# Asking earlier for the tables, spectra and filter of a convolution that runs beside an FFN, with tables and planes in common buffers

## The chip, the cores and the metric

The kernel runs on one core of a Trainium2 chip. The metric is the device time of one execution in microseconds (us); lower is better. A core has five engines that run at the same time and wait for each other through semaphores: TensorE (PE, matrix products), VectorE (DVE), ScalarE (ACT), GpSimd (POOL) and SyncE (SP), which here only issues DMAs. POOL also issues DMAs. PE's weight loads have a row of their own in the profile (PEld).

## The reference

Two blocks follow each other. The first is a long convolution by FFT with an implicit filter (batch 4, sequence 12544, 128 channels); the second is a maxout FFN over all 50176 tokens:

```python
h_filt = (np.maximum(pos_emb @ w1, 0) @ w2) * np.exp(-0.01 * pos)[:, None]
u = x * v
Uf = np.fft.rfft(u, n=2 * S, axis=1)
Hf = np.fft.rfft(h_filt, n=2 * S, axis=0)
y = np.fft.irfft(Uf * Hf[None], n=2 * S, axis=1)[:, :S]
z = (x * y).reshape(B * S, D)                       # D = 128
h = np.maximum(np.maximum(z @ m1, z @ m2), z @ m3)  # d_ff = 768
out = h @ m_out
```

## The kernel before

**Stages.** The transform is split by hand into a short one over 90 frequencies and a long one over 128 points, written as fp32 matrix products. Until about 290 us the kernel computes the filter's spectrum (kept in HBM as `hd`) and convolves batch 0. Then comes a loop over the FFN tiles of batches 0, 1 and 2: 32 tiles a batch, each of 6 slots, so 192 slots a batch. In a slot PE computes one sixth of a tile's FFN (`up`, tile `hps`, then `down`, tile `ops`), and beside it runs a piece of the convolution of the *next* batch. The last batch's FFN, from about 1,770 us on, has nothing beside it.

**What runs beside the FFN.** `conv_steps` makes a plan by hand: a list of steps for each slot. First, in the slots up to about 53, come 32 *units* of the next batch: load (`u_load`, SP), multiply and cut into 16-bit planes (`u_mul`, `u_planes`, POOL), transpose by DMA (`u_dma`, SP), join, first transform (`u_two`, `u_fours`). They fill the tile `spec`. From slot `s0` (58 in batch 2's plan) on come the *pairs*: 45 frequency steps g, two to a start slot, a new pair each 5.1 slots or so. With s for the start slot of a pair:

- `w_load` (L506, DMA at L508 on POOL) brings the tables `wt` of one step, 256 KB; one table serves the forward step g and the inverse step g - 3.
- `q_load` (L512, L520 on SP) brings the spectra `sq` of the two steps of a pair, eight DMAs of 64 KB out of `spec`, two buffers.
- `h_load` (L526, L531 on SP) brings the filter `ht` of the two steps, four DMAs of 256 KB out of `hd`, two buffers.
- `g_quarter` (L537) in slot s: PE multiplies `sq` by `wt` (L547) and, for the inverse of g - 3, `xs` by `wt` (L557).
- `g_fold`, `q_swap`, `q_re`, `q_im`, `q_unfold` in the next slots: ACT, DVE and POOL make `cb` and `xs` of it; `q_re` and `q_im` (DVE, L596) multiply by `ht`, and POOL adds at L599. `q_im` of a pair's second step has, in most pairs, the slot s + 5.
- `g_store` (L580, POOL) writes the inverse step's result to HBM (`zd`).

**Order of the queues.** Each engine executes its instructions in the order in which the program emits them, slot by slot. SP's list holds, besides the above, `t_load` (L776): at each tile's first slot it asks for the tile after the next of `zt` out of `zd` (L782 for batch 0, L789 after it; two buffers), and its first DMA waits until that buffer is read out. On each of the two DMA queues a DMA also waits for the landing of the one eight places before it, whose semaphore it takes over. POOL's list holds the tables' DMAs, the stores of `zd` and of the FFN's output (`ot`), the loads of `xT` and the sums at L599.

The asking steps stand in the plan at these slots: tables and spectra at s - 4, the filter at s - 1. The first pairs have entries of their own (`h_load` of the first two pairs, `w_load` of the first three tables).

Of the kernel before, what the change touches and what calls it, by code (L numbers as in the profile page):

```python
# [10 lines left out]
FP32 = mybir.dt.float32  # L11
I32 = mybir.dt.int32
U16 = mybir.dt.uint16
# [3 lines left out]
P = 128  # L17
# [78 lines left out]
def kernel(  # L96
# [21 lines left out]
    NK = N1 // 2  # L118
# [287 lines left out]

    def u_planes(u):
        a, _ = us.pop(u)
        pl_ = cvp.tile([P, 2, 4, P], U16, tag="pl", name="planes", bufs=3)
        w = pl_[:].rearrange("p h s (e m) -> p h s e m", e=2)  # L410
        nc.gpsimd.memset(pl_[:].rearrange("p h s (e m) -> p (h s e) m", e=2)[:, :, HB:], 0)
        for h in range(2):
            nc.gpsimd.tensor_copy(  # L413
                w[:, h, :, :, 0:HB],
                a[:].bitcast(U16).rearrange("p s (m e h) -> p h s e m", e=2, h=2)[:, h])
        us[u] = pl_
# [87 lines left out]
            fn()  # L504

    def w_load(x):  # L506
        w = wp.tile([P, 2, 2, 2, 64], FP32, tag="w", name="wt")
        nc.gpsimd.dma_start(w[:].rearrange("p a k r m -> p (a k r m)"),  # L508
                            wq_d[x].rearrange("p a f -> p (a f)"))
        ws[x, 0], ws[x - LATE, 1] = w[:, 0], w[:, 1]  # L510
# [153 lines left out]
    def conv_steps(b, done):  # L664


        out = []

        def at(slot, late, fn, *args):
            out.append((slot, late, len(out), fn, args))  # L670

        for u in range(5, done):
            at(2 * (u - 4), 1, u_first, u)
        lead, low, UNIT = (-14, -NT * NF, 0.8) if b > 1 else (6, 0, 0.7)
        share = UNIT * (NU - done - 1)
        per_pair = (END - lead - 11) / (share + (NK + LATE) // 2 * 2 - 2)
        units = []
        for u in range(done, NU):  # L680
            s = (u - done) * UNIT * per_pair + lead
            load_ = max(low, int(s) - 9)
            at(load_, 0, u_load, b, u)
            mul = max(load_ + 2, int(s) - 6)
            at(mul, 0, u_mul, u, nc.gpsimd)
            at(max(mul, int(s) - 5), 0, u_planes, u)
            at(max(mul + 1, int(s) - 4), 0, u_dma, u)
            at(int(s), 0, u_join, u)
            if u % 2:
                on = int(s + 2)  # L690
                at(on, 1, u_two, u - 1)
                at(on + 1, 1, u_fours, u - 1)
                at(on + 2, 1, u_fours, u)
                units.append(on)
        s0 = on + 7

        def start(x):
            return s0 + int(x // 2 * 2 * per_pair)

        load = [0.6] * (NT * NF)  # L700
        for x in range(NK + LATE):
            s = start(x)
            load[s] -= 1.2
            load[s + 1 + x % 2] += 1.4

        def emptiest(among, cost):
            s = min(among, key=lambda i: load[i])
            load[s] += cost
            return s

        plan = []
        busy = {start(x): 2 for x in range(NK + LATE)}
        for x in range(NK + LATE):
            busy.setdefault(start(x) + 1, 1)
        for s in units:
            for k, n in enumerate((1, 3, 9, 2)):
                busy[s - 1 + k] = max(n, busy.get(s - 1 + k, 0))
        for i in range(NT - 1):
            s = i * NF
            last = min((3, 4, 2), key=lambda k: busy.get(s + k, 0))  # L720
            load[s + last] += 0.6
            if s <= s0:
                plan.append((0, 0, last))
                continue
            a = emptiest(range(s, s + 2), 0.7) - s
            plan.append((a, emptiest(range(s + a, s + max(a + 1, last - 1)), 0.7) - s, last))
        plan.append((3, 3, 4))

        for at_, fn, *args in ((11, h_load, 0, 2), (10, h_load, 2, 2),
                               (9, w_load, 0), (9, w_load, 1), (8, w_load, 2)):  # L730
            at(s0 - at_, 0, fn, *args)
        for x in range(NK + LATE):
            s, odd = start(x), x % 2
            g, z = x if x < NK else None, x - LATE if x >= LATE else None
            at(s, 1, g_quarter, g, z)
            at(s + 1 + odd, 0, g_fold, g, z)
            if x > 2:
                at(s - 4, 0, w_load, x)
            if z is not None:
                at(s + 3 + odd, 0, g_store, b, z)  # L740
            if g is None:
                continue
            if g % 2 == 0:
                at(s - 4, 0, q_load, g, min(2, NK - g))
                if g > 2:
                    at(s - 1, 0, h_load, g, min(2, NK - g))
            first = s + 2 + 2 * odd
            at(first, 0, q_swap, g, 0)
            at(first + 1, 0, q_swap, g, 64)
            last = start(x + LATE) - 1  # L750
            a = emptiest(range(first + 1, min(first + 3, last - 1) + 1), 0.7)
            at(a, 0, q_re, g)
            a = emptiest(range(a, min(first + 4, last - 1) + 1), 0.7)
            at(a, 0, q_im, g)
            two = sorted(emptiest(range(a + 1, last + 1), 0.55) for _ in range(2))
            for q in range(2):
                at(two[q], 0, q_unfold, g, q)
        slots = {}
        for s, _, _, fn, args in sorted(out, key=lambda r: r[:3]):
            slots.setdefault(s, []).append((fn, args))  # L760
        return slots, plan, s0
# [288 lines left out]
    for u in range(4, NU, 2):  # L1050
        t = uts.pop(u)
        for v in range(2):
            if u + 4 < NU:
                u_mul(u + 4 + v)
            at = 4 * (u + v)
# [23 lines left out]
    cvp = pro.enter_context(tc.tile_pool(name="cvp0", bufs=3))  # L1079
# [94 lines left out]
    for s in range(NK + 3):  # L1174
# [34 lines left out]
        if s == NK:  # L1209
            unit(0)  # L1210
            pl = sps.tile([P, 512], FP32, tag="pl", name="pl")
# [23 lines left out]
    wp = conv.enter_context(tc.tile_pool(name="wp", bufs=3))  # L1235
    hh = conv.enter_context(tc.tile_pool(name="hh", bufs=2))
    cvp = conv.enter_context(tc.tile_pool(name="cvp", bufs=3))
# [12 lines left out]
    for b in range(1, B):  # L1250
        slots, *rest = conv_steps(b, EARLY if b == 1 else 0)
        plans.append(rest)
        for s, steps in slots.items():
            besides.setdefault((b - 1) * NT * NF + s, []).extend(steps)
# [145 lines left out]
```

## Time and profile before

| | |
|---|---|
| time, median of 3 runs | 2230.89 us (2227.69, 2230.89, 2235.35) |
| profiled execution | 2221.21 us, its span 2219.4 us |
| PE busy | 2194.1 us, 99% of the span |
| DVE, ACT, POOL busy | 1534.6, 1210.9, 1179.0 us |
| loop over the FFN tiles of batches 0 to 2 | about 290 to 1,770 us of the span |
| pairs run in | 447 to 768, 952 to 1,263 and 1,457 to 1,768 us |

All times within the execution count from the start of the span. The profiled execution is one execution with the hardware's profiler on; it took 9.7 us less than the median of the runs without it. A row of a view of waits reads: engine, tile and line that waited, then who ended the wait, the total in us, how many times, and the longest.

### The profile page before, as it was taken

To read this page: it belongs to the slowest core of one execution; us is meant where nothing else is said; L and a number is where in the kernel's file an instruction comes from. 1 tells how busy PE (TensorE), PEld (TensorE's weight loads), DVE (VectorE), ACT (ScalarE), POOL (GpSimd) and SP (SyncE) were. 2 spreads that over 40 slices of the span, in tenths; PEclk is the share of its full clock that TensorE was granted. 3 is DMA by queue.
4 is the path that set the end of the run, shared out by engine and by line. 5 is a ranking of instruction groups with operands and counts; after the bars stand their busy time and mean duration, and the time that the engine had idled before them with its cause. 6 is when DMAs were issued, how large, how long until landed. Compare 5 with 4: busy or idle time off the path is not lost.

```text
span 2219.4 us, 77166 instructions
## 1 busy us (share of the span) xinstructions
PE 2194.1 (99%) x31655; PEld 1297.3 (58%) x31655; DVE 1534.6 (69%) x3293; ACT 1210.9 (55%) x2223; POOL 1179.0 (53%) x1577
## 2 busy tenths in 40 slices
PE   9999999999999999999999999999999999999999
PEld 7988755555555455555555555555555545667776
DVE  5688857677877766667888766677878744554443
ACT  3699845466666555456666555556666622222222
POOL 1166567534455566544444566634454426666665
PEclk9999999999999999999999999999999999999999
DMA  8789999879999898879999999969999722222221
GB/s 196 186 264 311 291 181 196 171 191 233 247 246 241 218 188 175 168 175 245 230 256 231 229 195 178 173 158 252 236 240 238 200 79 58 59 71 69 63 58 24
DMA packets 491332, 411.62 MB, mean 185 GB/s; under 512 B 289406, under 2 KB 407920, under 8 KB 490979
## 3 DMA queue, kind: packets, MB, share of 16 engines
q1 hardware_dynamic: 443689, 274.50, 56.6%
q0 software_dynamic: 45808, 130.25, 21.5%
q8 instruction: 249, 4.08, 0.8%
q10 hardware_dynamic: 1482, 1.93, 0.4%
q14 instruction: 104, 0.85, 0.1%
HBM read 262.85 MB, written 84.67 MB: 157 GB/s over the span
## 4 chain that ended last, share of the span: by engine, by line
PE 84%; DMA 6%; DVE 3%; POOL 3%; issue 2%; SPq 1%; ACT 1%; POOLq 0%; DVEq 0%; ACTq 0%
PE hps L167 42%; PE ops L167 17%; PE ops L903 6%; PE cps L167 3%; PE cps L449 3%; PE ps L176 3%; PE cps L547 3%; PE cps L557 2%; DMA sq<-spec 2%; DMA ht<-hd 2%; DMA zt<-zd 1%; PE ps L167 1%; DMA wt<-wq_const 1%; POOL xt L638 1%; PE last L167 1%
## 5 line engine op out<-in xcount | busy, mean ns | idle before, releaser
L167 PE MATMUL hps<-gt,w_sb 128*64 128x392 f32 (+1 forms) x7672 | 1157.4, 495 | 0.8 <-DVE gt L829 0.7
L839 ACT ACTIVATE hid<-hps 128x392 f32<-128x392 f32 x768 | 382.5, 498 | 762.7 <-PE hps L167 744.9
L167 PEld LDWEIGHTS hps<-gt,w_sb 128*64 128x64 f32 (+1 forms) x7672 | 430.6, 126 | 439.1 <-issue 407.9
L842 DVE TENSOR_TENSOR hid<-hid,hps 128x392 f32<-128x392 f32 x768 | 427.8, 557 | 351.5 <-PE hps L167 335.8
L167 PE MATMUL ops<-hid,wo_sb 128*64 128x392 f32 x2304 | 476.9, 492 | 0.0
L599 POOL TENSOR_TENSOR cb<-cb,xs 128x512 f32<-128x512 f32 x135 | 177.4, 1314 | 404.9 <-DVE xs L596 389.5
L167 PEld LDWEIGHTS ops<-hid,wo_sb 128*64 128x64 f32 x2304 | 165.7, 137 | 213.5 <-issue 213.5
L572 DVE TENSOR_TENSOR cb<-cps,eo 128x512 f32<-128x512 f32 (+1 forms) x288 | 175.1, 649 | 72.8 <-ACT eo L569 71.7
L857 POOL DMA_DIRECT2D out_dram<-ot x96 | 76.3, 795 | 235.3 <-ACT ot L855 217.2
L587 ACT ACTIVATE xs<-cb 32x512 f32<-32x512 f32 x270 | 169.4, 628 | 21.5 <-DVE cb L572 12.6
L588 ACT COPY xs<-cb 32x512 f32<-32x512 f32 x270 | 166.3, 616 | 3.2
L603 DVE TENSOR_TENSOR xs<-cb 128x256 f32<-128x256 f32 x270 | 148.7, 598 | 6.5 <-POOL cb L599 6.5
L429 ACT COPY uT<-turned 113x512 uint16<-113x512 uint16 x180 | 126.0, 771 | 0.1
L386 POOL TENSOR_TENSOR ut<-ut 128x392 f32<-128x392 f32 x90 | 93.3, 1037 | 41.2 <-DMA ut<-in_vr_dram 39.2
L167 PEld LDWEIGHTS cps<-f4p,even 90*64 90x64 f32 x1552 | 87.2, 138 | 35.9 <-issue 33.2
L772 POOL DMA_DIRECT2D xT<-in_x_dram x172 | 101.1, 601 | 6.8 <-PE pt L1099 3.3
L580 POOL DMA_DIRECT2D zd<-cb x135 | 95.0, 704 | 14.6 <-DVE cb L572 10.7
L471 DVE TENSOR_TENSOR low<-high,cps 128x180 f32<-128x180 f32 x186 | 54.6, 334 | 67.6 <-ACT high L461 67.6
L928 POOL DMA_DIRECT2D out_dram<-o x120 | 72.5, 610 | 47.2 <-DVE o L921 45.7
L167 PE MATMUL cps<-f4p,zt 90*64 90x49 f32 x1552 | 95.8, 222 | 0.0
L547 PE MATMUL cps<-sq,wt 64*64 64x128 f32 x2160 | 90.6, 276 | 4.6 <-DMA wt<-wq_const 2.9
L413 POOL COPY planes<-ut 128x392 uint16<-128x392 uint16 x180 | 95.1, 564 | 0.0
(172 smaller groups left out, 3348.2 us busy)
## 6 DMA issues: line engine op xcount, KB each, us to landing
ht<-hd SPq DMA_DIRECT2D x264, 256.0 KB, 7.1
wt<-wq_const POOLq DMA_DIRECT2D x144, 256.0 KB, 5.3
zd<-cb POOLq DMA_DIRECT2D x135, 256.0 KB, 6.3
zt<-zd SPq DMA_DIRECT2D x384, 90.0 KB, 3.8
sq<-spec SPq DMA_DIRECT2D x528, 64.0 KB, 5.6
ut<-in_xr_dram SPq DMA_DIRECT2D x128, 196.0 KB, 4.3
ut<-in_vr_dram SPq DMA_DIRECT2D x128, 196.0 KB, 4.5
wt<-wt_const SPq DMA_DIRECT2D x90, 256.0 KB, 5.1
```

What stands on the lines that cost most here:

```text
L167: nc.tensor.matmul(out[h:h + w], lhsT[:, h:h + w], rhs, start=start, stop=stop, skip_group_check=True)
L429: nc.scalar.copy(uts[u][0:HR, 8 * (u % 2):8 * (u % 2) + 8].rearrange("n s r t -> n (s r t)").bitcast(U16).rearrange("n (s r t h) -> n h s ...
L547: nc.tensor.matmul(ps[64 * a:64 * a + 64, at:at + D], w[64 * r:64 * r + 64, k, a, :], t[64 * r:64 * r + 64, k, :, a], start=(k == 0), stop ...
L572: nc.vector.tensor_tensor(out=cb[:, a, lo:hi], in0=ps[:, lo:hi], in1=eo[:, lo:hi], op=op)
L587: nc.scalar.mul(xs[at:at + 32], xt[at + 32:at + 64], -1.0)
L588: nc.scalar.copy(xs[at + 32:at + 64], xt[at:at + 32])
L599: nc.gpsimd.tensor_tensor(out=xts[g], in0=xts[g], in1=xs[:], op=ALU.add)
L603: nc.vector.tensor_tensor(out=ab[:, q], in0=y[:, 0], in1=y[:, 1], op=(ALU.subtract, ALU.add)[q])
L772: eng.dma_start(xT[c * NG:(c + 1) * NG].rearrange("d i p n -> d (i p) n"), x[:, 4 * i:4 * i + 8, c, b, :])
L839: nc.scalar.activation(h[:], pa[:, 0:N], Relu)
L842: nc.vector.tensor_tensor(out=h[:], in0=h[:], in1=pb[:, 0:N], op=ALU.max)
L903: nc.tensor.matmul(ps[32 * q:32 * q + 32, 0:H2], w[:, m:m + 32], rhs[:, H2 * c:H2 * c + H2], start=start, stop=True, skip_group_check=True)
```

## The change

Tables and spectra of a pair are asked for at s - 6 in place of s - 4 (the first pair's spectra stay at s - 4), the filter at s - 3 in place of s - 1. The tables had three buffers of their own (pool `wp`, tag `w`, 2 KB a partition each); the units' planes had three buffers of the same size (tag `pl`). Now both take turns in six buffers under the tag `pl`, so the memory used is the same.

```diff
     def u_planes(u):
         a, _ = us.pop(u)
-        pl_ = cvp.tile([P, 2, 4, P], U16, tag="pl", name="planes", bufs=3)
+        pl_ = cvp.tile([P, 2, 4, P], U16, tag="pl", name="planes", bufs=6)
...
     def w_load(x):
-        w = wp.tile([P, 2, 2, 2, 64], FP32, tag="w", name="wt")
+        w = cvp.tile([P, 2, 2, 2, 64], FP32, tag="pl", name="wt", bufs=6)
...
             at(s, 1, g_quarter, g, z)
             at(s + 1 + odd, 0, g_fold, g, z)
             if x > 2:
-                at(s - 4, 0, w_load, x)
+                at(s - 6, 0, w_load, x)
...
             if g % 2 == 0:
-                at(s - 4, 0, q_load, g, min(2, NK - g))
+                at(s - (6 if g else 4), 0, q_load, g, min(2, NK - g))
                 if g > 2:
-                    at(s - 1, 0, h_load, g, min(2, NK - g))
+                    at(s - 3, 0, h_load, g, min(2, NK - g))
```

The instructions of PE, DVE and ACT and their order stay as they are. SP's and POOL's instructions are the same in kind and number; in their order the asking steps stand two slots earlier.

## The prediction

> **What bounds the kernel now.** I read the page's head first, then the waits of PE over the stages with pairs, the timeline around three pairs, then the queues.
>
> ```profile
> span 2219.4 us, 77166 instructions
> PE 2194.1 (99%) x31655; PEld 1297.3 (58%) x31655; DVE 1534.6 (69%) x3293; ACT 1210.9 (55%) x2223; POOL 1179.0 (53%) x1577
> ```
>
> PE has almost no idle time and its instructions stay as they are, so the change can only take away what PE waits for. Waits of PE from 440 to 1,780 us:
>
> ```profile
> PE cps L547 <- DMA wt<-wq_const: 2.9, 4, 1.3
> PE cps L547 <- DMA sq<-spec: 1.4, 5, 0.5
> PE cps L557 <- DVE xs L603: 0.5, 2, 0.3
> ```
>
> Nine waits for just the two transfers that are asked for earlier, 4.3 us. A row counts only from the modelled end of the previous matmul, so I measured the loss on the timeline: from the start of the FFN's `ops` ahead of a pair to the start of the next `hps`. An undisturbed pair, one that waits for `sq` and one that waits for `wt`:
>
> ```profile
> 1057.06 0.83 PE L167 MATMUL ops<-hid,wo_sb 128*64 128x392 f32 x4
> 1059.72 1.54 PE L167 MATMUL hps<-gt,w_sb 128*64 128x392 f32 x8
> ...
> 1030.05 0.83 PE L167 MATMUL ops<-hid,wo_sb 128*64 128x392 f32 x4
> 1031.71 0.54 PE L547 MATMUL cps<-sq,wt 64*64 64x128 f32 x10 [0.46 <-DMA sq<-spec]
> 1033.61 1.54 PE L167 MATMUL hps<-gt,w_sb 128*64 128x392 f32 x8
> ...
> 715.76 0.83 PE L167 MATMUL ops<-hid,wo_sb 128*64 128x392 f32 x4
> 718.96 0.67 PE L547 MATMUL cps<-sq,wt 64*64 64x128 f32 x16 [1.34 <-DMA wt<-wq_const]
> 720.00 1.54 PE L167 MATMUL hps<-gt,w_sb 128*64 128x392 f32 x8
> ```
>
> The distances are 2.66, 3.56 and 4.24 us. Read so for the 60 pairs g = 4 to 42 of the three batches, 49 show 2.67 us to the hundredth and 11 are longer. The pairs at 525, 716 and 1,099 us lose 1.67, 1.58 and 1.04 us, with `wt` named: 4.3 us. The other eight wait for `sq` and lose 0.06 to 0.89 us: 4.6 us. Together **8.9 us**, twice the row's figure; it is all that the change can win in this execution.
>
> Why they come late is read from SP's waits from 1,000 to 1,240 us and from the windows:
>
> ```profile
> SPq L520 <- DMA ht<-hd: 41.1, 57, 2.7
> SPq L789 <- DMA sq<-spec: 13.4, 17, 1.9
> SPq L789 <- PE cps L167: 8.3, 4, 4.3
> ...
> 200.00:250.00 50.00, 48.90 (x1032) 43.24 (x1030) 44.23 (x118) 46.96 (x87) 32.39 (x43) 1.00 1.00 329
> 1000.00:1240.00 240.00, 239.00 (x2770) 125.82 (x2768) 195.28 (x348) 156.20 (x281) 115.78 (x148) 1.00 0.97 243
> ```
>
> `sq` does not read `ht`: that wait is for the DMA eight places before. So SP keeps eight DMAs under way, and is held besides by `zt`'s buffer (L789 behind PE). A pair takes 13.5 us (5.1 slots of 2.65 us) and SP issues 8 + 4 + 4 x 5.1/6 = 15.4 DMAs in it; eight at a time that works while a landing takes under 8 x 13.5 / 15.4 = **7.0 us**. Medians are 5.7 (`sq`), 6.8 (`ht`) and 5.0 (`zt`): stable, but with little to catch up with. Granted clock: 1.00 in all these windows.
>
> **The change, part by part.** *Tables.* Two slots are 5.3 us. POOL works in order, and ahead of the tables' new place stands the sum (L599) of slot s - 7. It ends some 4.7 us after that slot's start (DVE's L596 ended 3.4 us after it where I looked, plus 1.3 us for the sum), so about s - 5.2: POOL can issue from there. Before, the tables at 1,023.83 us came 7.0 us (2.6 slots) ahead of their pair at 1,030.81. The gain in lead lies between 0 (if POOL is held by a store of `ot`, whose longest wait is 9.9 us) and 6.9 us; I take 4 us, nearest to that working. The largest wait for a table is 1.34 us, so the 4.3 us go. The two DMAs cost POOL 2 x 0.57 us ahead of the next sum; POOL idles 389.5 us at L599 anyway, so nothing, and 1.1 us of delay to a sum if that cover were gone.
>
> *Spectra.* The step 12 at 1,030.81 us: its `sq` were issued from 1,018.20 on and landed at 1,031.7. In the new order they stand ahead of the `zt` they followed, and behind `h_load` of step 10. That one takes a **new wait**: its buffer is read by `q_im` of step 7, two slots before the new place in the program where there were four. This is the L596 that ended at 1,007.05 us. Four issues of `ht` at 0.5 us end at 1,009, so `sq` can start 9 us earlier at best; at the least 0, if the eight places are all taken. The two slots of the plan, 5.3 us, lie between, and I take 5. The eight take 7 us to issue as before, so they land near 1,026.7, 4 us early. The longest loss by `sq` is 0.89 us. I count 0.5 us for one pair in each start of a stretch, where SP has still to catch up. So 4.6 - 0.5 = 4.1 us go.
>
> *Filter.* DVE has no row of waiting for `ht`, so its earlier landing wins nothing. Queued behind the new wait on SP are the next `zt` and the next `sq`. `zt` is next late if SP slips: those landed by 1,186.5 us were first read at 1,196.7, the smallest margin in that stretch's middle, 10 us against a group of eight `sq` (7 us) that now goes ahead of some of them. Hidden; without that cover a `zt` late by 1 us would cost PE 1 us.
>
> *Common buffers.* Six buffers in turn: a table takes the one of three pairs ago, read long before. The three waits "POOL wt L508 <- PE cps L547: 20.2" at the first pairs go; PE had no wait there, so 0. POOL's next there is a sum at L599, which waits for DVE. Bounds of this edit: 0 to 0.7 us (PE's waits for `xs`, 0.37 us lost at each of two stretch ends), taken at 0.
>
> Sum for the profiled execution: 2221.21 - 4.3 - 4.1 = **2212.8 us**. The median lies 9.7 us higher; the same 8.4 us make 2222.5. PE repeats itself to 0.01 us wherever nothing is late, so part of what the unprofiled runs take longer may be more of the same waits, which would go too. I have no row for it; it sets the low end, 2230.9 - 8.9 - 9.7 = 2212.3.
>
> *A rule against it.* The engines' share is 0.97 in the stretch with pairs, at 243 GB/s; while the filter was made the same 16 moved 329 GB/s at 1.00. So there is room, if the packets allow it. The Trainium skill's page "DMA: Bandwidth & Descriptors", section "Issuing engines are not separate DMA queues", says that DMAs from SP and GpSimd share the same 16 engines and interleave. By that rule an earlier `sq` only takes its share from `wt`, `zd` and `ht`, and with full engines the sum would be near 2230.9. By the rows it is 2222.5.
>
> **Rivals.**
> 1. *The earlier `sq` do not land earlier* (engines full, or the change does not do what it says because SP is held at `h_load`). For: the 41.1 us on `ht` show a full list of eight. Against: SP also idles for `zt`'s buffer, 29.4 us from 440 to 770 us, time that earlier places can use. Then only the tables' 4.3 us go: 2226.6, no measurable change.
> 2. *Slower: the list of eight tips over.* SP now stands at `h_load` until DVE has done `q_im`, then sends `ht` and `sq` close together. If landings rise over 7.0 us, SP falls behind each pair by 15.4/8 = 1.9 times the excess, until PE waits. The loss after the won 8.9 us decides from (8.9 + 6.7)/63 = 0.25 us a pair on (63: 23 pairs in each of three batches without the first two). With 0.3 us: 2230.9 - 8.9 + 18.9 = 2240.9. For: landings of 8 to 10 us stand in the trace in bursts. Against: the sums of bytes are the same, and from 1,045 to 1,090 us SP held its lead without any loss.
> 3. *Larger waits in the runs without profiler:* 2212 to 2217, the forecast's own low side.
>
> **How the numbers follow.** A measurement of this kernel can tell about 0.3%, 6.7 us. Forecast with rival 3: 0.65, of which a little stays under 6.7 us (8.4 is not far from it), so 0.61 faster. Rival 1: 0.22, and with that remainder 0.26 within 0.3%. Rival 2: 0.13. The range reaches from the low end above to the upper part of no change, 2232.
>
> **What would show it.** Right: no row of L547 behind `wt` or `sq`, at most one or two short ones at the first pairs of a stretch; all 60 distances at 2.67 us; a new row "SPq L531 <- DVE xs L596" in SP's waits; no row "POOL wt L508 <- PE". Step by step wrong: rows for `sq` stay while those for `wt` go (rival 1); median landings over 7 us and new rows of `zt` or `sq` at most pairs (rival 2). The forecast fails altogether if those rows go and the time does not.

## The result: 13.8 us faster, and the profile after

| | before | changed |
|---|---|---|
| median of six runs | 2230.47 us (2227.69 to 2239.71) | 2216.69 us (2215.36 to 2219.41) |
| profiled execution, its span | 2221.21 us, 2219.4 us | 2216.71 us, 2214.9 us |

The ratio is 0.9941 with a 95% interval of 0.9927 to 0.9956: faster, by 13 us at the ratio and 13.8 us at the medians. The forecast was 2222.5 us, with 2212 to 2232 as its range. The measured time lies at the low side of the range, where the prediction put its rival 3 (2212 to 2217 us). The two profiled executions lie only 4.5 us apart; the changed kernel's equals its median, before's was 9 us below its own.

The view of PE's waits from 440 to 1,780 us, of the changed kernel:

```profile
PE cps L547 <- DMA sq<-spec: 2.3, 2, 1.5
PE cps L557 <- DVE xs L603: 0.5, 2, 0.3
```

The row for `wt` is gone, and of the waits for `sq` two are left. Neither is one of before's. PE's timeline of the changed kernel, at the pair that was shown late before (3.56 us), and then at the first pair of the second stretch:

```profile
1030.03 0.83 PE L167 MATMUL ops<-hid,wo_sb 128*64 128x392 f32 x4
1030.79 0.67 PE L547 MATMUL cps<-sq,wt 64*64 64x128 f32 x16
...
1032.69 1.54 PE L167 MATMUL hps<-gt,w_sb 128*64 128x392 f32 x8
```

```profile
949.88 0.83 PE L167 MATMUL ops<-hid,wo_sb 128*64 128x392 f32 x4
950.64 0.43 PE L547 MATMUL cps<-sq,wt 64*64 64x128 f32 x4
952.54 1.09 PE L547 MATMUL cps<-sq,wt 64*64 64x128 f32 x28 [1.47 <-DMA sq<-spec]
953.57 0.88 PE L167 MATMUL hps<-gt,w_sb 128*64 128x392 f32 x4
```

1032.69 - 1030.03 is 2.66 us, and within a hundredth so it is at 59 of the 60 pairs (the sixtieth loses 0.09 us): 8.9 us lost at these pairs have become 0.2, about half of which is the last digit of 60 distances. But at the first pairs of two stretches PE now waits for `sq`, where before it did not: the same distance is 953.57 - 949.88 = 3.69 us here and 3.01 us at 448 us, against 1.79 us at all three first pairs of before, so 3.1 us in all. How SP got its lead, from its timeline:

```profile
1007.41 2.46 SPq L531 DMA_DIRECT2D ht<-hd  x4
1010.87 6.13 SPq L520 DMA_DIRECT2D sq<-spec  x8
1017.43 2.52 SPq L789 DMA_DIRECT2D zt<-zd  x4
```

The spectra of the pair at 1,030.8 us are issued from 1,010.87 on (before: 1,018.20), right behind the filter, and ahead of the `zt` that stood ahead of them before. The last of them landed at 1,020.0 us (before: 1,031.7).

A measure that leaves the first 450 us out is the time from PE's first product of a pair to the end of the span. Those 450 us alone differ by some 3 us between executions (first product at 446.3 to 449.1 us over the profiles below that start at this slot). It was 1772.1 us before and 1766.4 us after. The same in each stretch, from its step 4 to its step 44: 271.2, 271.7 and 272.1 us before; 266.9, 269.7 and 269.7 us after.

### The profile page after: what moved, and what is told of

It reads as the page before. It is cut to its first block, busy times and chain, and to the rows that moved or that the text cites. A ratio compares the mean times of both kernels' runs of the same rounds, so it can differ in the third digit from the quotient of the medians.

```text
span 2214.9 us, 77203 instructions
## 1 busy us (share of the span) xinstructions
PE 2191.9 (99%) x31655; PEld 1295.4 (58%) x31655; DVE 1533.7 (69%) x3293; ACT 1211.1 (55%) x2223; POOL 1180.0 (53%) x1577
## 4 chain that ended last, share of the span: by engine, by line
PE 91%; DVE 3%; POOL 2%; issue 2%; DMA 1%; ACT 1%; SPq 1%; POOLq 0%; ACTq 0%; DVEq 0%
PE hps L167 46%; PE ops L167 19%; PE ops L903 6%; PE cps L167 4%; PE cps L547 3%; PE cps L449 3%; PE ps L176 3%; PE cps L557 3%; PE ps L167 1%; POOL xt L638 1%; PE last L167 1%; DVE ab L645 1%; DVE xs L637 1%; PE ps L391 1%; POOL specH L638 1%
## 5 line engine op out<-in xcount | busy, mean ns | idle before, releaser
L599 POOL TENSOR_TENSOR cb<-cb,xs 128x512 f32<-128x512 f32 x135 | 177.6, 1316 | 368.3 <-DVE xs L596 345.6
L167 PE MATMUL cps<-f4p,even 90*64 90x49 f32 x1552 | 94.6, 220 | 0.0
```

What stands on the lines that cost most here:

```text
L167: nc.tensor.matmul(out[h:h + w], lhsT[:, h:h + w], rhs, start=start, stop=stop, skip_group_check=True)
L599: nc.gpsimd.tensor_tensor(out=xts[g], in0=xts[g], in1=xs[:], op=ALU.add)
```

## The experiments

The theory is that the time lies in PE's waits for `wt` and `sq` alone, and that ordinary executions of before hold more of them than the profiled one did. The rivals: one of the two moves does it all; the common buffers do it, through POOL's freed waits; the filter's place does it by spreading the requests. All ratios are to the kernel before, run on the same chip among the runs of the same study. "Lost at the pairs" is read from the timeline as in the prediction, for the same 60 pairs.

**Before against itself**, with no edit.

> The kernel before, unchanged, against itself, with a second profile. Theory (waits): an ordinary execution of it holds more waits of PE for sq and wt than the profiled one did, so this profile, if its span is near 2228 us, shows about 16 us lost at the pairs in place of 8.9. Rival (other cause): the span is longer by time in the first 290 us or spread over all stages, and the pairs lose 8 to 10 us as before. The ratio should be 1.000 within 0.002.

Measured: ratio 1.0009 (0.9995 to 1.0024), span of the profiled execution 2216.4 us, 5.2 us lost at 12 pairs (0.04 to 0.97 us each). Only some of the late pairs are those of the first profile: 525 us lost 1.67 and now 0.09 us, while 1,601 us went from nothing to 0.97. So the same program, instruction for instruction, loses 5.2 us in one execution and 8.9 in another: landings differ, PE's own work does not. From the first pair to the end it took 1768.5 us, 3.6 less than the first profile, against 3.7 us less lost. The expected 16 us were forecast for a span near 2228 us and could not be tested, since this execution was again a short one.

**Only the tables earlier** (and the common buffers that this needs).

```diff
-                at(s - (6 if g else 4), 0, q_load, g, min(2, NK - g))
+                at(s - 4, 0, q_load, g, min(2, NK - g))
-                    at(s - 3, 0, h_load, g, min(2, NK - g))
+                    at(s - 1, 0, h_load, g, min(2, NK - g))
```

(against the changed kernel)

> Only the tables two slots earlier, with the six common buffers; spectra at s - 4 and filter at s - 1 as before. Theory (waits): the waits for wt go and those for sq stay, about half of the gain, some 6 to 7 us (ratio 0.997). Rival (tables alone): the whole gain of 13 us (0.994). Rival (spectra alone): no gain (1.000).

Measured: ratio 0.9975 (0.9963 to 0.9986), 5.8 us at the medians, as the theory expected. 2.2 us are lost at the pairs, nearly all by `sq`, and 3.8 us at the three first pairs. In its profile PE waits for `sq` alone (both places together):

```profile
PE cps L547 <- DMA sq<-spec: 3.6, 4, 1.1
```

The changed kernel gained 13.8, 10.1 and 7.4 us in the three studies that had it, so the tables bring a good part of the gain; how large a part is not shown, as no study had both. Fewer pairs than before lose by `sq`, which was not expected. The spectra were asked for no earlier (15.6 us ahead of their pair in the median, 15.9 before) and landed no earlier (3.3 us ahead in both), so this can be a difference between executions, as between the two profiles of before.

**Only the spectra earlier.**

```diff
-                at(s - 4, 0, q_load, g, min(2, NK - g))
+                at(s - (6 if g else 4), 0, q_load, g, min(2, NK - g))
```

(against before)

> Only the spectra two slots earlier; tables at s - 4 in their own three buffers, filter at s - 1. Theory (waits): the waits for sq go and those for wt stay or are uncovered a little, since both were late at the same pairs: 5 to 7 us gained (ratio 0.997). Rival (spectra alone): the whole 13 us (0.994). Rival (tables alone): nothing.

Measured: ratio 0.9991 (0.9978 to 1.0003), unclear; 14.4 us lost at the pairs in the profile. PE's waits in it:

```profile
PE cps L547 <- DMA wt<-wq_const: 8.6, 11, 2.4
PE cps L547 <- DVE xs L596: 0.8, 1, 0.8
```

No row for `sq` is left, and `wt` has grown from 2.9 us in 4 waits to 8.6 in 11. It is tempting to say that the one wait had only hidden the other. The traces do not show that: at ten of the twelve late pairs `sq` had landed 4 us or more ahead, by the landings that can be told, and `wt` alone was late, as it was at 525, 716 and 1,099 us before; the tables are asked for as early as before (8.7 us ahead of the pair in the median); and the profile with only the filter earlier, below, has 7.4 us of `wt` too. So how much is lost by `wt` differs between executions. What the run shows is that waits for `sq` went and that this gained nothing measurable. The prediction's rival 1 does not hold: the spectra did land earlier, some 6 us ahead of their pair in the median in place of 3.3.

**Only the common buffers.**

```diff
-                at(s - 6, 0, w_load, x)
+                at(s - 4, 0, w_load, x)
```

(against the kernel with only the tables earlier)

> Only the common buffers; all asking steps at the slots of before. Theory (waits): POOL's three waits of 6.7 us for PE at the first pairs go, PE's waits stay: no gain (1.000 within 0.002). Rival (buffers): POOL's freed 20 us reach PE, and some 5 us or more are gained (0.998 or less).

Measured: ratio 1.0016 (1.0005 to 1.0026), slower by about 3.5 us at the ratio and 2.6 at the medians. POOL's row for the wait on PE is gone, and the gain that the rival hoped for does not come. 16.5 us were lost at the pairs in this execution (2233.7 us, the longest of its twelve), and the first pairs of all three stretches wait for `sq` and lose 0.4, 1.3 and 1.4 us. Every profile with common buffers and this start has such waits in two or three stretches; no profile of a kernel with the buffers apart and spectra at s - 4 or s - 6 has it. POOL's timelines around the second stretch's first pair show what differs, first before, then the changed kernel:

```profile
945.88 0.78 POOL L857 DMA_DIRECT2D out_dram<-ot  x1 [8.85 <-ACT ot L855]
953.49 0.54 POOL L508 DMA_DIRECT2D wt<-wq_const  x1 [6.84 <-PE cps L547]
954.07 2.34 POOL L772 DMA_DIRECT2D xT<-in_x_dram  x4
```

```profile
944.02 0.78 POOL L857 DMA_DIRECT2D out_dram<-ot  x1 [8.86 <-DMA sq<-spec]
944.79 0.54 POOL L508 DMA_DIRECT2D wt<-wq_const  x1
945.32 2.34 POOL L772 DMA_DIRECT2D xT<-in_x_dram  x4
```

Before, the fourth table and four loads of `xT` had to wait at POOL until the first pair was through PE. Now they go out from 944.8 us on, while the last of the first pair's `sq` are on their way (issued until 945.7). That last one landed in 6.7 us; in before the eighth took 3.8. SP asked for the first pair's spectra 9.57 us ahead of the pair in both, so the lead is the same and the landing is what differs. What looked like a useless wait had, it seems, kept the DMA engines free; that the five DMAs of POOL are what delayed `sq` is read from their coming together, and no run moved them alone.

**The changed kernel among its parts**, and **the change without its filter part**, from one study.

> The changed kernel once more, beside the parts. Theory (waits): span = some 2211 us without any wait plus what PE loses at the pairs; this one loses 0 to 1 us at the pairs and about 3 us at the first pairs of the stretches, so 2214 to 2215 us of span again, whatever before takes. If before takes 2224 us here, the ratio is 0.996; if 2230 us, 0.993. Rival (other cause): the ratio of the first measurement, 0.994, stays whatever before takes.

```diff
-                    at(s - 3, 0, h_load, g, min(2, NK - g))
+                    at(s - 1, 0, h_load, g, min(2, NK - g))
```

> The change without its filter part: tables and spectra at s - 6, common buffers, filter still at s - 1. Theory (waits): the filter's place matters only as what stands on SP between two groups of spectra; without its new wait for DVE nothing holds SP, so the time is as with the change, within 2 us (ratio to before as for the changed kernel, within 0.001). Rival (filter): the filter's earlier place spreads the requests, and without it some of the waits for sq come back, 3 us or more.

Measured: 0.9957 (0.9943 to 0.9970) and 0.9958 (0.9945 to 0.9971); spans 2212.8 and 2214.6 us; lost at the pairs 0.2 us in both. The filter's earlier place does nothing measurable beside the other two. Before took 2226.1 us in the median here, 4.4 us less than in the first measurement, and the changed kernel 2216.0, 0.7 less: it is before that differs between the studies, as the theory expected (0.996 if before takes 2224 us), and not a fixed ratio of 0.994.

**Only the filter earlier.**

```diff
-                    at(s - 1, 0, h_load, g, min(2, NK - g))
+                    at(s - 3, 0, h_load, g, min(2, NK - g))
```

(against before)

> The kernel before with only the filter earlier (s - 3). Theory (waits): nothing waits for ht, and four DMAs of 256 KB now stand closer behind a pair's spectra and ahead of a zt: 0 to 4 us slower than before (1.000 to 1.002), with the waits for sq and wt as they were. Rival (filter): the earlier filter makes room for the next spectra, and 3 us or more are gained.

Measured: ratio 1.0001 (0.9991 to 1.0011). No difference; 12.9 us lost at the pairs in the profiled execution, most of it by `wt`, whose place was not changed:

```profile
PE cps L547 <- DMA wt<-wq_const: 7.4, 9, 1.6
PE cps L547 <- DMA sq<-spec: 0.6, 2, 0.3
```

**The other way: tables and spectra one slot later than before.**

```diff
-                at(s - 4, 0, w_load, x)
+                at(s - 3, 0, w_load, x)
-                at(s - 4, 0, q_load, g, min(2, NK - g))
+                at(s - 3, 0, q_load, g, min(2, NK - g))
```

> The other way: the kernel before with tables and spectra asked for at s - 3 in place of s - 4 (filter at s - 1, own buffers). Theory (waits): a lead shorter by 2.6 us, and before had 0 to 4 us to spare at most pairs, so about half of the 63 pairs wait 1 to 2 us: 30 to 60 us lost at the pairs, ratio 1.010 to 1.025. Rival (the engines' share, not the lead): transfers land when their turn comes; the same 5 to 16 us as before, ratio 1.00.

Measured: ratio 1.0063 (1.0046 to 1.0079), 26.8 us lost at 19 of the 60 pairs. The sign is right, and the size is below what was expected (30 to 60 us and a ratio of 1.010 to 1.025). A slot in the plan is 2.65 us, but it was not 2.65 us of lead: at the 60 pairs the spectra were asked for 14.7 us ahead in the median in place of 15.9, and the tables 8.5 us in place of 8.7. What stands ahead of them on SP and POOL decides that; which step held them was not looked for. In its profile PE waits:

```profile
PE cps L547 <- DMA wt<-wq_const: 14.7, 12, 3.0
PE cps L547 <- DMA sq<-spec: 2.9, 6, 0.8
```

**All pairs one slot later**, on the changed kernel, against the new wait at the first pairs.

```diff
-        s0 = on + 7
+        s0 = on + 8
```

> The changed kernel with the pairs started one slot later (s0 = on + 8 in place of on + 7), so that the first pair's spectra, which cannot be asked for before the last units have written them, have 2.6 us more. Theory (waits): the waits of 1.0 to 1.8 us at the first pair of each stretch go: 2 to 3 us faster than the changed kernel (0.999 of it), span 2211 to 2213 us. Rival: the first pair is held by something that moves with it, and nothing changes; or the tail of the stretch, now one slot later, runs into the next batch and loses as much.

Measured: ratio 0.9952 (0.9938 to 0.9965); span 2212.2 us. The waits at the first pairs are gone, and in their place PE waits 2.3 us for `xs` at the two ends of stretches, at 756 and 1,260 us, where it waited 0.5: the rival's second half.

**Only the first pairs one slot later**: up to the first gap of six slots in the plan, so that a stretch's end stays.

```diff
-        s0 = on + 7
+        s0 = on + 8
...
-            return s0 + int(x // 2 * 2 * per_pair)
+            slots = [int(2 * k * per_pair) for k in range(x // 2 + 1)]
+            return s0 + slots[-1] - any(q - p > 5 for p, q in zip(slots, slots[1:]))
```

> The changed kernel with only the first pairs one slot later: s0 = on + 8, and from the plan's first gap of six slots on all starts as in the changed kernel, so that the end of each stretch is not moved. Theory (waits): the waits for sq at the first pairs go, the waits for xs at the end stay as in the changed kernel (0.4 us each): 2 to 3 us less than the changed kernel, 2211 us of span or less. Rival: the first pair is held by something that moves with it; no gain.

> The changed kernel a third time, as the measure for the three beside it: span 2212 to 2215 us, 0 to 0.5 us lost at the 60 pairs, some 2 to 3 us at the first pairs of the stretches.

Measured on one chip: this version 2213.81 us, ratio 0.9959 (0.9946 to 0.9971), span 2212.0 us; the changed kernel 2215.64 us, ratio 0.9969 (0.9957 to 0.9981), span 2215.3 us. In the stretches with pairs the view of PE's waits now has one row left:

```profile
PE cps L557 <- DVE xs L603: 0.5, 2, 0.3
```

It has the lowest median of all kernels here. By the intervals it beats before clearly; the 1.8 us by which it beats the changed kernel are less than the 2 to 3 us expected and lie within the overlap of the two intervals, so they are likely and not shown.

**Still earlier: tables and spectra at s - 8.**

```diff
-                at(s - 6, 0, w_load, x)
+                at(s - (8 if x > 5 else 6), 0, w_load, x)
-                at(s - (6 if g else 4), 0, q_load, g, min(2, NK - g))
+                at(s - (8 if g > 2 else 6 if g else 4), 0, q_load, g, min(2, NK - g))
```

> The changed kernel with tables and spectra asked for at s - 8 from the third pair on (filter still at s - 3). Theory (waits): the pairs wait for nothing any more with s - 6, so there is nothing left to win: within 1 us of the changed kernel. Rival (more lead is better): the last 2 to 3 us go too. If it is slower, the new order on SP (spectra right behind the filter) makes zt or ht late.

Measured: ratio 0.9970 (0.9960 to 0.9981), 2216.39 us, 0.2 us lost at the pairs: the same as the changed kernel beside it. With s - 6 the lead is enough.

All profiles in which the pairs begin at the same slot, in the order of what PE lost at the 60 pairs. The third column is read as the second, at the three first pairs (distances over 1.79 us):

| kernel | lost at the pairs, us | lost at the first pairs, us | first pair to the end, us |
|---|---|---|---|
| changed (three profiles) | 0.2, 0.2, 0.2 | 3.1, 3.0, 2.6 | 1766.4, 1766.4, 1767.4 |
| without filter part; at s - 8 | 0.2; 0.2 | 2.0; 3.4 | 1765.5; 1767.1 |
| tables alone | 2.2 | 3.8 | 1770.3 |
| before (two profiles) | 5.2, 8.9 | 0, 0 | 1768.5, 1772.1 |
| filter alone | 12.9 | 0 | 1777.1 |
| spectra alone | 14.4 | 0 | 1777.9 |
| common buffers alone | 16.5 | 3.1 | 1783.9 |
| one slot later | 26.8 | 0.8 | 1792.8 |

The last column less the other two lies between 1763.1 and 1765.2 us for all of them. The five above 1764 us are two with a wait of PE of some 1 us at L449 (the third profile of the changed kernel, tables alone) and three in which the clock fell between 440 and 1,780 us (filter alone, common buffers, one slot later; see the last section). So what differs between these kernels, and between two executions of one, is what PE loses at its pairs and first pairs.

## Why the prediction was right, and where it was off

*The bound.* PE's waits for `wt` and `sq` were what the change could take, and the distances on the timeline were the right way to size them: 8.9 us, with the rows of waits telling 4.3. They went to 0.2.

*Tables.* A lead 4 us longer was taken, between 0 and 6.9. At the step shown the tables are issued at 1,017.59 us, 13.2 us ahead of the pair in place of 7.0: 6.2 us more, near the upper bound. That step is not typical: over the 60 pairs the median went from 8.7 to 12.9 us, 4.2 us more, so the weighing was right, and so was the conclusion (all of the 4.3 us).

*Spectra.* 5 us earlier were taken, of at most 9, with a landing near 1,026.7. At the step shown it was 7.3 us, and the landing at 1,020.0. Here the step flatters: over the 60 pairs the median went from 15.9 to 19.4 us, 3.5 us more, so 5 was too much, and the last landing came 6.4 us ahead of the pair in the median in place of 3.3. That was enough, as no loss by `sq` had been over 0.89 us. For the starts of the stretches, where SP has still to catch up, the prediction counted 0.5 us for a pair in each (1.5 for three), but took only 0.5 off its sum. Some waits did stay there, but 3.1 us, at the first pairs themselves, and for another reason.

*Filter.* The new wait came as foreseen, in SP's waits of the changed kernel from 440 to 770 us:

```profile
SPq L782 <- PE hps L167: 17.3, 11, 5.1
SPq L531 <- DVE xs L596: 16.8, 10, 5.0
```

It took over 12 us of the 29.4 that SP had waited there for `zt`'s buffer, and nothing behind it came late: no row of a wait for `zt` or `ht` stands in PE's or DVE's waits from 440 to 1,780 us. It was of no measurable use either.

*Common buffers: the step that failed.* They were put between 0 and 0.7 us of gain and taken at 0. "PE had no wait there, so 0" was true of the waits of before, but with POOL's wait gone the changed kernel's profile loses 3.1 us at the first pairs, and alone this edit costs 3.5 us by the ratio. The prediction named as POOL's next step there a sum at L599 that waits for DVE. Before's timeline, shown above, has the fourth table and four loads of `xT` ahead of it; these went out earlier and met the first pair's `sq`.

*The size.* 8.4 us were forecast and 13.8 measured. For the profiled execution 2212.8 us were forecast, and it took 2216.7. The sum over the pairs holds there: from the first pair to the end 5.7 us were won, 8.7 at the pairs less 3.1 at the first pairs. These 3.1 us are most of the miss, and 1.3 us lie ahead of the first pair. The rest is that before's ordinary executions are longer than its profiled one (2230.5 against 2221.2 us) and the changed kernel's are not (2216.7 both). The prediction gave this as its low side and its rival 3, without a row for it. The table makes it likely: two profiles of before differ by what they lose. So does the granted clock of the 35 runs of before beside the first experiments: the runs at 0.998, 0.997, 0.996 and 0.995 took 2220.9, 2222.8, 2225.4 and 2227.7 us in the median, as runs with more long waits would. It is not shown, since no profile of before at 2230 us was caught. In the two later comparisons before took 2226.1 and 2223.1 us, and the changed kernel was faster by 10.1 and 7.4 us, so 13.8 us is the largest of three gains, and the 8.4 us forecast lie among them. In the first comparison two errors of the forecast have opposite signs, the cost at the first pairs and the longer executions of before; that it fell inside the range with both is in part luck.

*The rule on shared engines.* By the Trainium skill's page "DMA: Bandwidth & Descriptors", section "Issuing engines are not separate DMA queues", the DMAs of all issuing engines run on the same 16 engines and interleave; the prediction drew from it that an earlier request only takes another's share. The windows from 1,000 to 1,240 us, of the changed kernel, show 244 GB/s (243 before) and PE without a gap.

```profile
1000.00:1240.00 240.00, 240.00 (x2782) 126.25 (x2780) 196.13 (x350) 157.11 (x283) 117.59 (x150) 1.00 1.02 244
```

As much is moved as before, which fits the rule, and the loads of `xT` landed later, as by the rule something would. The DMA views of this window, before and then changed (the last number is the median time to landing):

```profile
xT<-in_x_dram POOLq DMA_DIRECT2D x28, 98.0 KB, 5.4
xT<-in_x_dram POOLq DMA_DIRECT2D x28, 98.0 KB, 8.1
```

The medians of the other kinds moved by 0.7 us or less, and nothing that PE waits for was pushed over its time, so it cost nothing here. The median landings on SP's queue are 6.0 (`sq`), 6.6 (`ht`) and 6.0 us (`zt`), under the 7.0 at which the list of eight would have tipped over (rival 2). Where more than a dozen DMAs met within a few microseconds, at the first pairs, one that PE did wait for came late, and that cost the 3.1 us.

## What to carry to other kernels

Where an engine is at 99% and repeats itself to the hundredth of a microsecond, measure its losses by the distance between two instructions that frame the waiting place, and do it in two executions: the rows of waits told half of them, and two profiles of the same program differed by 3.7 us. Read a lead at all pairs and not at one: the step shown had 6.2 us more where the median had 4.2. Where a step needs two requests, look at which of the two is late: moving the spectra alone left the time where it was, moving the tables alone won 5.8 us. Before a wait on a side engine is taken away, look at which transfers stand behind it, and who is on the DMA engines when they are let go.

## What the runs showed of the hardware

A long wait of PE can cost more than its length. In the kernel with only the common buffers PE stood idle for 2.75 us at 1,035 us, and the pair lost 3.7 us; the `hps` behind it took 2.65 us, where it takes 1.54 behind an undisturbed pair:

```profile
1037.95 0.55 PE L547 MATMUL cps<-sq,wt 64*64 64x128 f32 x10 [2.75 <-DMA sq<-spec]
1040.36 2.65 PE L167 MATMUL hps<-gt,w_sb 128*64 128x392 f32 x8
```

The windows behind the wait (the columns after PE's busy time are weight loads, DVE, ACT and POOL, then the granted clock, the engines' share and GB/s):

```profile
1038.00:1040.00 2.00, 2.00 (x58) 2.00 (x60) 0.00 (x0) 0.00 (x0) 1.81 (x3) 0.81 1.08 254
1040.00:1043.00 3.00, 3.00 (x17) 1.17 (x14) 0.00 (x0) 0.97 (x2) 0.00 (x0) 0.56 1.07 280
1043.00:1046.00 3.00, 3.00 (x22) 1.26 (x18) 2.33 (x4) 1.50 (x3) 0.00 (x0) 1.00 0.60 158
```

These are means over the windows: in the trace the granted clock is 0.50 from 1,039.24 to 1,042.66 us, 3.41 us long, and 1.00 on both sides. The length of a wait alone does not decide whether it falls. It fell to 0.50 for 3.41 us after 1.43 us of idle time at 622 us (and 0.20 us shortly before) with only the filter earlier, and stayed at 1.00 after 3.00 us at 625 us in the kernel with its requests one slot later. The Trainium skill's page "TensorE: Matmul & The Clock Gate", section "What's actually happening", lets the clock fall to half after an idle window of about 3.4 us and calls this window free-running. The step of 3.41 us agrees with that, and so does a wait's place mattering beside its length; but the idle times of 2.75 and 1.43 us are shorter than a window, so here one with some matmuls in it was enough.

A share of the DMA engines near 1 did not tell how much they moved: at 0.97 to 1.02 they moved 243 to 244 GB/s in these stretches, and at 1.00 to 1.01 329 to 331 GB/s between 200 and 250 us.
